# Gated recurrence and ELU layer in one kernel: VectorE's sums read two phases' banks straight from PSUM, and what follows them is put in another order

## The chip, the core and the metric

One core of one Trainium2 chip runs the kernel. Its engines run side by side, each through its own list of instructions in order: TensorE (PE, with its weight loads as PEld), VectorE (DVE), ScalarE (ACT), GpSimd (POOL) and SyncE (SP), which only issues transfers here. The metric is the time of one execution on the device in microseconds (us). Matrix products land in PSUM, eight banks of 128 x 512 fp32 numbers. All else lies in SBUF.

## The reference

For 4 batches, 8 heads, 768 tokens and a head width of 48, a state is carried along the tokens, and its output, 3072 rows of 384 numbers, goes through a two-layer network with an ELU between:

```
f = 1 / (1 + exp(-f_logit))
state = 0
for t in range(768):
    state = f[t][:, None] * state + outer(k[t], v[t])
    y[t] = q[t] @ state
x = y as 3072 x 384
h = x @ w_in                                  # 384 x 2048
g = where(h > 0, h, exp(min(h, 0)) - 1)
out = g @ w_out                               # 2048 x 384
```

w_in and w_out arrive as 64-bit floats. The kernel makes fp32 weights of them and also checks their range, since a fast way and a general way share one launch and a flag chooses at the end which result stands.

## The kernel before

The 3072 tokens are worked off in 12 **units** of 256. Units 0 and 1 use plain first products, while the weights are being converted and summed. Units 2 to 11 use a scheme with fewer products, and this is where the change lies.

**A unit in the network.** The 2048 hidden columns are split into four **quads** of 512. A quad's eight blocks of h (four column blocks by two token blocks, each 128 x 128) come out of 20 products of 128 x 128 instead of 24. Each product multiplies a block of x, or a sum of such blocks, by a block of w_in, or a sum of such blocks; the h blocks are then sums and differences of the products. The sums of x blocks (`X_SUMS`, made by `blend`, L939) are made on POOL for each unit from unit 3 on: slots 0 to 7 of the tile `xt` hold x, and the sums fill slots 8 to 15 and then write over some of the first eight. `PHASES` splits a quad's 20 products into five **phases** of 3, 5, 5, 4 and 3 products (tile `psH`, L957). A phase adds into one of the quad's two banks; its last number lists the products as (slot of the bank, slot of x, block of w). After each phase ScalarE copies what is complete into the tile `vals` (L962), 18 blocks of 128 x 128 of which there are two, one for even and one for odd quads. VectorE makes the h blocks from `vals` in seven additions of 128 x 256 (`joins`, L947): four after phase 3, three after phase 4. The two banks go round: the first bank of the next quad is the second bank of this one, and so the next quad's phase 0 waits until phase 3 of this one has been read, and its phase 1 until phase 4 has been.

**ELU and the second product.** A **pair** is half a quad: 256 hidden columns for 256 tokens, eight pairs a unit, two a quad. For a pair ScalarE runs Relu and Exp into a tile `gg` (L970, L971) and VectorE one fused operation that completes the ELU (L990). POOL makes four sums of 128 x 128 from it (tile `sums`, L1000), and PE seven products of 128 x 192 into `psM` (L1049). After a unit's eighth pair VectorE combines the banks of `psM` (L1059) and SP stores.

**The attention** of unit u+1 or u+2 is worked off beside it: ScalarE makes the gates, VectorE scans and reciprocals (L685, L690), POOL scales k and q by them (L680), PE has short products (`psT`, `psU`, `psS`, `psY`), VectorE masks (L776) and adds up states (L749), ScalarE copies the unit's x into `xt` (L837, L839).

**What sets the order.** It is written out by hand. The loop at the end runs over **steps** of two phases each, ten a unit, here called s0 to s9; time T counts half steps. In each step it issues what `plan` holds for T, the two phases and their joins, what `plan` holds for T + 1, some products of the second layer (`take`, as many as `CHUNKS` says), and the exponentials of a pair. Before the change, the ELU operations due come first in a step; a quad that ends in step s has the exponentials of its first pair at the end of step s and of its second at the end of s + 1, and each pair's ELU at the start of the step after. Quads end in s2, s4, s7 and s9. `BL`, `A3`, `D4` place a unit's x sums, attention and decays within the unit before. Each engine's list is the order of issue, so an instruction waits for all that was issued to its engine before it. All waits between engines are semaphores for data or buffers.

Of the kernel before, what the change touches and what calls it, by code (L numbers as in the profile page):

```python
# [8 lines left out]
FP32 = mybir.dt.float32  # L9
# [3 lines left out]
AF = mybir.ActivationFunctionType  # L13
# [343 lines left out]
def fast(ctx: ExitStack, tc: tile.TileContext, q, k, v, f_logit, w_in, w_out, out, flag, outer):  # L357
# [53 lines left out]
    A3 = (3, 7, 11, 13)  # L411
    BL = 15
# [5 lines left out]
        (14, 1, 5, -1), (12, 1, 0, -1), (1, 3, 1, -1), (9, 2, 3, -1), (13, 4, 9, -1), (8, 2, 4, -1),  # L418
        (10, 2, 0, -1), (7, 8, 14, -1), (2, 13, 5, -1), (11, 10, 9, -1), (15, 0, 14, -1), (6, 4, 15, -1),
# [14 lines left out]
    )  # L434
    SEED = (1, 5)
    JOIN3 = (
        (ALU.add, (5, 12), (7, 17), (11, 12)), (ALU.add, (4, 17), (15, 15), (4, 13)),
        (ALU.add, (5, 13), (5, 6), (10, 12)), (ALU.subtract, (7, 14), (11, 13), (8, 14)),
    )
    JOIN4 = (  # L440
        (ALU.add, (8, 15), (0, 1), (3, 12)), (ALU.add, (7, 16), (7, 16), (8, 9)),
        (ALU.subtract, (6, 17), (8, 13), (2, 17)),
    )
    PLACES = ((14, ((1, 1), (1, 0), (0, 0), (0, 1))), (4, ((1, 1), (0, 1), (1, 0), (0, 0))))
# [89 lines left out]
    vals = [cst.tile([128, 18, 128], FP32, name=f"vals{i}") for i in range(2)]  # L534
# [121 lines left out]
    def check(n):  # L656

        if not wide:
            return
        hi = again.pop(n)[:].bitcast(FP32)[:, 1::2]  # L660
        for i, op in enumerate((ALU.min, ALU.max)):
            nc.vector.tensor_reduce(
                out=spans[:, i, n : n + 1], in_=hi, axis=mybir.AxisListType.X, op=op, apply_absolute_value=True
            )
# [270 lines left out]
    def blend(u, e, some=slice(None)):  # L935

        x = xts[u]
        for to, a, b, _ in X_SUMS[some]:
            e.tensor_tensor(out=x[:, to], in0=x[:, a], in1=x[:, b], op=ALU.subtract)  # L939
# [3 lines left out]
    def joins(n, todo):  # L943
        v = vals[n % 2]
        pick = lambda a, b: v[:, a : b + 1 : b - a] if b > a else v[:, a : a + 1].broadcast_to([128, 2, 128])
        for op, to, x, y in todo:
            nc.vector.tensor_tensor(out=pick(*to), in0=pick(*x), in1=pick(*y), op=op)  # L947

    def phase(n, i):
# [12 lines left out]
        nc.scalar.copy(v[:, at : at + size], bank[:, frm : frm + size])  # L962
# [3 lines left out]
    def exped(P, h, where):  # L966
        m, j = order[P]
        g = sb.tile([128, 4, 128], FP32, tag="gg", name=f"gg{m}_{j}", bufs=4)
        gs[P] = g, where
        nc.scalar.activation(g[:], h, AF.Relu, scale=-1.0)  # L970
        nc.scalar.activation(g[:], g[:], AF.Exp, scale=-1.0)  # L971
        phs[P] = h
# [14 lines left out]
    def elu(P):  # L987
# [5 lines left out]
        if m > DIRECT or m == DIRECT and j >= PLAIN:  # L993
            s = ss[P] = sb.tile([128, 4, 128], FP32, tag="sums", name=f"sums{m}_{j}", bufs=3)
# [89 lines left out]
    def finish_flag(part):  # L1084
        if wide and not part:
            ok = fine[:, 0, 0:1]
            nc.vector.tensor_reduce(out=spans[:, 0, 0:1], in_=spans[:, 0], axis=mybir.AxisListType.X, op=ALU.min)
            nc.vector.tensor_reduce(out=spans[:, 1, 0:1], in_=spans[:, 1], axis=mybir.AxisListType.X, op=ALU.max)
            for i, op, limit in ((0, ALU.is_ge, 1.125 * 2.0**-15), (1, ALU.is_lt, 1.875 * 2.0**16)):
# [124 lines left out]
    at_step(BL2, lambda: blend(2, nc.vector, slice(0, 6)), lambda: blend(2, nc.gpsimd, slice(6, 12)))  # L1214
# [46 lines left out]
    CHUNKS = (6, 6, 6, 0, 7, 6, 6, 6, 7, 6)  # L1261

    def exp_pair(n, i):
        frm, where = PLACES[i]
        exped(PLAIN_UP * NP + 2 * n + i, vals[n % 2][:, frm : frm + 4], where)
# [25 lines left out]
    for n, z in exps.pop(5 * total // 2):  # L1291
        exp_pair(n, z)
        elus.setdefault(5 * total // 2 + 1, []).append(lambda n=n, z=z: elu(PLAIN_UP * NP + 2 * n + z))
    for s in sorted(elus):
        for f in elus[s]:
            f()
# [51 lines left out]
```

## Time and profile before

| | |
|---|---|
| runs of the kernel | 624.70, 626.36, 629.08 us; median 626.36 |
| the profiled execution | 624.47 us, its span 622.7 us, mean granted TensorE clock 0.963 |
| units 0 and 1 | until about 120 us |
| units 2 to 11 | from there to the end; the same wait of PE comes back at 168.98, 219.01, ... 368.73, 418.03, ... 516.46, 564.22 us, so a unit takes about 49.4 us |
| busy between 368 and 418 us | PE 44.2, DVE 36.0, ACT 25.9, POOL 28.7 us |
| SP's list | transfers alone |

In the rows of the trace, a matrix product of fp32 numbers stands as two records, and a record is about 0.29 us long, though the next one starts 0.11 or 0.16 us after it: the pace of PE is read from stretches of many records. "L957" is line 957 of the kernel before; the same code stands a few lines further down in the changed one.

### The profile page before, as it was taken

The page shows a single profiled execution, that of the slowest core. Times are in us where ns is not written, and L with a number is a line of the kernel's source. Part 1 is how long each engine was busy: PE and PEld are TensorE (multiplying, and loading weights), DVE is VectorE, ACT ScalarE, POOL GpSimd, SP SyncE. Part 2 cuts the span into 40 slices and gives each one's busy share as a digit, 9 for nine tenths or more (in the row PEclk, how much of TensorE's full clock was granted, in tenths as well). Part 3 has the DMA queues.
Part 4 walks back from the last instruction along what each step waited for, and adds up shares of the span by engine and source line. Part 5 has one row for each costly group of instructions (what it writes and reads, how often), then busy time and mean ns, then how long its engine had stood idle before and what let it go on. Part 6 is the DMA issues. An engine that isn't in the chain of part 4 may idle for free.

```text
span 622.7 us, 15560 instructions
## 1 busy us (share of the span) xinstructions
PE 554.0 (89%) x6294; PEld 510.2 (82%) x6294; DVE 442.0 (71%) x757; ACT 318.9 (51%) x595; POOL 326.4 (52%) x603
## 2 busy tenths in 40 slices
PE   7799999798799889979979889988989988998994
PEld 3477688788798789879869879878879987997993
DVE  8889776967657858767856866776785786754652
ACT  3387933345455634745527535645554473564541
POOL 6603173665842862672583493485386276355342
PEclk9999999989889989989979989999998997999998
DMA  9999840130142062062061133215206202210001
GB/s 207 256 223 274 229 116 2 33 102 22 36 117 78 8 171 78 8 171 79 9 152 48 50 78 108 72 26 153 78 8 172 78 7 65 78 34 1 27 3 31
DMA packets 39474, 54.29 MB, mean 87 GB/s; under 512 B 4032, under 2 KB 29216, under 8 KB 39392
## 3 DMA queue, kind: packets, MB, share of 16 engines
q1 hardware_dynamic: 38592, 52.61, 32.4%
q8 instruction: 51, 0.84, 0.6%
q10 hardware_dynamic: 800, 0.59, 0.4%
q14 instruction: 31, 0.25, 0.1%
HBM read 45.02 MB, written 4.72 MB: 80 GB/s over the span
## 4 chain that ended last, share of the span: by engine, by line
PE 38%; DVE 26%; POOL 13%; ACT 10%; issue 6%; DMA 6%; SPq 1%; ACTq 0%; DVEq 0%; POOLq 0%
PE psM L1049 14%; PE psH L957 14%; DVE vals L947 13%; POOL xt L939 9%; PE psH L980 3%; DVE gg L990 3%; POOL sums L1000 3%; ACT gg L970 2%; DMA f<-f 2%; DVE f L690 2%; ACT vals L962 2%; DVE f L685 2%; ACT gg L971 2%; PE psS L768 1%; PE psU_a L791 1%
## 5 line engine op out<-in xcount | busy, mean ns | idle before, releaser
L1000 POOL TENSOR_TENSOR sums<-gg 128x128 f32<-128x128 f32 x172 | 83.3, 504 | 203.9 <-DVE gg L990 189.4
L947 DVE TENSOR_TENSOR vals<-vals 128x256 f32<-128x256 f32 x280 | 142.1, 519 | 67.0 <-ACT vals L962 59.2
L962 ACT COPY vals<-psH 128x512 f32<-128x512 f32 (+1 forms) x200 | 105.1, 540 | 122.7 <-PE psH L957 121.5
L957 PE MATMUL psH<-xt,wi 128*128 128x128 f32 x880 | 144.7, 286 | 3.5 <-DVE gg L990 3.5
L957 PE MATMUL psH<-xt,area 128*128 128x128 f32 x720 | 128.0, 283 | 12.1 <-ACT vals L962 11.0
L1049 PE MATMUL psM<-area,sums 128*128 128x192 f32 x516 | 112.5, 343 | 28.0 <-POOL sums L1000 28.0
L957 PEld LDWEIGHTS psH<-xt,wi 128*128 128x128 f32 x880 | 125.5, 202 | 3.7 <-DVE gg L990 3.7
L957 PEld LDWEIGHTS psH<-xt,area 128*128 128x128 f32 x720 | 107.7, 197 | 15.7 <-ACT vals L962 13.7
L1049 PEld LDWEIGHTS psM<-area,sums 128*128 128x128 f32 x516 | 89.1, 200 | 31.1 <-POOL sums L1000 31.0
L970 ACT ACTIVATE gg<-vals 128x512 f32<-128x512 f32 x80 | 50.4, 630 | 104.7 <-DVE vals L947 76.0
L990 DVE SCALAR_TENSOR_TENSOR gg<-gg,vals 128x512 f32<-128x512 f32 x80 | 58.2, 728 | 59.6 <-ACT gg L971 51.7
L1049 PE MATMUL psM<-wo,gg 128*128 128x192 f32 x376 | 80.5, 336 | 10.2 <-DVE gg L990 10.2
L1049 PEld LDWEIGHTS psM<-wo,gg 128*128 128x128 f32 x376 | 62.4, 191 | 16.0 <-DVE gg L990 15.2
L939 POOL TENSOR_TENSOR xt<-xt 128x128 f32<-128x128 f32 x114 | 59.9, 553 | 9.2 <-DMA xt<-xt 3.9
L690 DVE RECIPROCAL f<-f 128x256 f32<-128x256 f32 x36 | 62.8, 1747 | 1.1
L971 ACT ACTIVATE gg<-gg 128x512 f32<-128x512 f32 x96 | 60.5, 630 | 3.1
L680 POOL TENSOR_TENSOR k<-k,f 128x256 f32<-128x256 f32 x48 | 37.5, 785 | 36.6 <-DVE f L685 16.1
L680 POOL TENSOR_TENSOR q<-q,f 128x256 f32<-128x256 f32 x48 | 39.0, 813 | 18.7 <-DMA f<-f 15.6
L1000 POOL TENSOR_TENSOR sums<-sums,gg 128x128 f32<-128x128 f32 x86 | 47.1, 548 | 0.0
L980 PE MATMUL psH<-xt,wi 128*128 128x256 f32 x192 | 45.1, 384 | 2.3 <-DVE xt L887 1.7
L1000 POOL TENSOR_TENSOR sums<-gg,sums 128x128 f32<-128x128 f32 x86 | 43.6, 507 | 6.7
L1049 PE MATMUL psM<-area,gg 128*128 128x192 f32 x172 | 43.9, 338 | 0.0
(107 smaller groups left out, 667.6 us busy)
## 6 DMA issues: line engine op xcount, KB each, us to landing
area<-in_moe_w_out_dram SPq DMA_DIRECT2D x8, 768.0 KB, 10.6
again<-in_moe_w_in_dram SPq DMA_DIRECT2D x16, 384.0 KB, 5.4
again<-in_moe_w_out_dram SPq DMA_DIRECT2D x16, 384.0 KB, 3.8
k<-in_k_dram SPq DMA_DIRECT2D x12, 384.0 KB, 4.7
q<-in_q_dram SPq DMA_DIRECT2D x12, 384.0 KB, 5.8
v<-in_v_dram SPq DMA_DIRECT2D x12, 384.0 KB, 6.0
area<-in_moe_w_in_dram SPq DMA_DIRECT2D x8, 576.0 KB, 9.2
out_dram<-o SPq DMA_DIRECT2D x42, 96.0 KB, 1.7
```

The lines of the kernel that those rows point to most:

```text
L680: e.tensor_tensor(out=t[n][:, p], in0=t[n][:, p], in1=t["f"][:, p, "kq".index(n)], op=ALU.mult)
L690: nc.vector.reciprocal(f[:, p, 1], f[:, p, 0])
L939: e.tensor_tensor(out=x[:, to], in0=x[:, a], in1=x[:, b], op=ALU.subtract)
L947: nc.vector.tensor_tensor(out=pick(*to), in0=pick(*x), in1=pick(*y), op=op)
L957: nc.tensor.matmul(bank[:, slot], lhsT=w_block(q, w), rhs=xts[m][:, x], start=(i < 2 and t == 0), stop=True, skip_group_check=True,)
L962: nc.scalar.copy(v[:, at : at + size], bank[:, frm : frm + size])
L970: nc.scalar.activation(g[:], h, AF.Relu, scale=-1.0)
L971: nc.scalar.activation(g[:], g[:], AF.Exp, scale=-1.0)
L980: nc.tensor.matmul(ph[:, i], lhsT=wi[j][:, kt, i * 128 : (i + 1) * 128], rhs=xts[m][:, 2 * kt : 2 * kt + 2].rearrange("n t f -> n (t f)"), ...
L990: nc.vector.scalar_tensor_tensor(out=g[:], in0=g[:], scalar=-1.0, in1=phs.pop(P), op0=ALU.add, op1=ALU.max)
L1000: nc.gpsimd.tensor_tensor(out=s[:, i], in0=x, in1=y, op=op)
L1049: nc.tensor.matmul(pm[bank][:, half * DH : (half + 1) * DH], lhsT=x, rhs=y, start=first, stop=(j == NP - 1), skip_group_check=True,)
```

## The change

- **Fewer copies.** ScalarE copies phases 0, 1 and 2 of a quad and no longer phases 3 and 4. VectorE's additions read these two phases' blocks in PSUM. There are eight additions a quad in place of seven: after phase 3 two of 128 x 256 and one of 128 x 128 with one operand in PSUM (`JOIN3`); after phase 4 one of 128 x 256 and one of 128 x 128 likewise (`JOIN4`); and three of 128 x 256 with both operands in SBUF (`MID`, two, and `LAST`, one). `PHASES`, `SEED` and `PLACES` are rewritten to suit; the sizes of the phases and the count of products stay. `vals` has 13 blocks in place of 18; `gg` has five buffers in place of four, `sums` four in place of three.
- **Order in a step.** The ELU operations come after the step's phases and joins, not ahead of them. Both pairs of a quad that ends in step s have their exponentials at the end of step s + 1 and their ELU in step s + 2. `CHUNKS` is changed with that; the first unit of the scheme takes 42 products of the second layer in its loop where it took 52, and what comes after the last step takes the rest.
- **Sums of x.** Twelve of 128 x 128 become six of 128 x 256, each making two sums. For units 3 to 11 they are issued one per half step from T = 16 to T = 21 after the start of the unit before (the last two in the unit's own first step), where all twelve came at T = 15.
- **Range checks.** Each of the 32 checks was two reductions of 128 x 384 on VectorE (least and greatest magnitude); it is now two activations on ScalarE that add up their results (squares, and an exponential that vanishes for all but tiny numbers), and `finish_flag` has other limits.

```diff
-    A3 = (3, 7, 11, 13)
-    BL = 15
+    A3 = (3, 9, 12, 13)
+    BL = 16
...
     X_SUMS = (
...
+        ((12, 13), (1, 2), (0, 0)), ((10, 11), (2, 2), (3, 4)), ((9, 14), (1, 4), (5, 10)),
+        ((1, 2), (3, 14), (1, 5)), ((8, 15), (0, 13), (9, 10)), ((6, 7), (4, 11), (8, 9)),
     )
...
     PHASES = (
...
+        (0, 1, 0, 3, ((1, 8, 16), (0, 9, 13), (2, 14, 12))),
+        (1, 8, 0, 4, ((0, 5, 4), (3, 3, 6), (1, 5, 14), (1, 1, 7), (2, 0, 15))),
+        (0, 4, 0, 4, ((1, 12, 20), (0, 7, 8), (2, 4, 18), (3, 13, 1), (3, 4, 2))),
+        (1, 0, 0, 0, ((0, 2, 19), (3, 1, 5), (1, 11, 0), (2, 15, 9))),
+        (0, 0, 0, 0, ((0, 6, 17), (2, 10, 11), (3, 13, 3))),
     )
...
     JOIN3 = (
...
+        (ALU.add, (4, 11), (4, 11), 1, (1, 2)), (ALU.add, (0, 12), (4, 9), 1, (0, 3)), (ALU.subtract, 4, 6, 1, 1, True),
     )
...
+    MID = (ALU.add, (1, 5), (1, 5), None, (9, 11)), (ALU.subtract, (8, 9), (5, 5), None, (8, 12))
+    JOIN4 = (ALU.add, (3, 6), (2, 11), 0, (0, 2)), (ALU.subtract, 2, 3, 0, 3)
+    LAST = ((ALU.add, (3, 7), (3, 10), None, (4, 7)),)
...
-        for i, op in enumerate((ALU.min, ALU.max)):
-            nc.vector.tensor_reduce(
-                out=spans[:, i, n : n + 1], in_=hi, axis=mybir.AxisListType.X, op=op, apply_absolute_value=True
-            )
+        nc.scalar.activation(hi, hi, AF.Square, accum_out=spans[:, 1, n : n + 1])
+        nc.scalar.activation(hi, hi, AF.Exp, scale=-(2.0**26), accum_out=spans[:, 0, n : n + 1])
...
-        nc.scalar.copy(v[:, at : at + size], bank[:, frm : frm + size])
+        if size:
+            nc.scalar.copy(v[:, at : at + size], bank[:, frm : frm + size])
...
-        at_step(t + BL, lambda u=u: blend(u, nc.gpsimd))
+        for n in range(6):
+            at_step(t + BL + n, lambda u=u, n=n: blend(u, nc.gpsimd, slice(n, n + 1)))
...
-    CHUNKS = (6, 6, 6, 0, 7, 6, 6, 6, 7, 6)
+    CHUNKS = (7, 7, 7, 7, 0, 6, 6, 6, 5, 5)
...
-        for f in elus.pop(s, ()):
-            f()
         for f in plan.pop(T, ()):
             f()
+        done = []
         for i in (2 * s, 2 * s + 1):
             n, i = divmod(i, 5)
             phase(n, i)
-            if i == 3:
-                joins(n, JOIN3)
-            elif i == 4:
-                joins(n, JOIN4)
-                for z in range(2):
-                    exps.setdefault(s + z, []).append((n, z))
+            if i > 2:
+                joins(n, JOIN3 if i == 3 else JOIN4)
+                done.append((n, MID if i == 3 else LAST))
+        for n, todo in done:
+            joins(n, todo)
+            if todo is LAST:
+                exps[s + 1] = n
+        for P in elus.pop(s, ()):
+            elu(P)
         for f in plan.pop(T + 1, ()):
             f()
-        take((5, 5, 4)[s] if s < 3 else CHUNKS[s % 10])
-        for n, z in exps.pop(s, ()):
-            exp_pair(n, z)
-            elus.setdefault(s + 1, []).append(lambda n=n, z=z: elu(PLAIN_UP * NP + 2 * n + z))
+        take((4, 4, 3, 3)[s] if s < 4 else CHUNKS[s % 10])
+        if s in exps:
+            exp_quad(exps.pop(s), s)
```

Three places show how the lists of the engines change; names end in the unit and, for `gg` and `sums`, the pair. The first is POOL's list around the start of unit 9 (unit 8 still being worked off): `xt9` are sums of unit 9's x blocks, `k0` and `q0` scalings for unit 10, `sums8_4` the sums that pair 4 of unit 8 needs. Before:

```order
L680 TENSOR_TENSOR q0_69<-q0_69,f0_68 128x256
L939 TENSOR_TENSOR xt9_4580<-xt9_4580 128x128 x12
L1000 TENSOR_TENSOR sums8_4_4630<-gg8_4_4626 128x128 x2
L1000 TENSOR_TENSOR sums8_4_4630<-sums8_4_4630,gg8_4_4626 128x128
L1000 TENSOR_TENSOR sums8_4_4630<-gg8_4_4626,sums8_4_4630 128x128
L680 TENSOR_TENSOR k0_70<-k0_70,f0_68 128x256
L680 TENSOR_TENSOR q0_69<-q0_69,f0_68 128x256
L1000 TENSOR_TENSOR sums8_5_4670<-gg8_5_4666 128x128 x2
L1000 TENSOR_TENSOR sums8_5_4670<-sums8_5_4670,gg8_5_4666 128x128
L1000 TENSOR_TENSOR sums8_5_4670<-gg8_5_4666,sums8_5_4670 128x128
```

After, the same place on POOL:

```order
L1005 TENSOR_TENSOR sums8_4_4592<-gg8_4_4569 128x128 x2
L1005 TENSOR_TENSOR sums8_4_4592<-sums8_4_4592,gg8_4_4569 128x128
L1005 TENSOR_TENSOR sums8_4_4592<-gg8_4_4569,sums8_4_4592 128x128
L1005 TENSOR_TENSOR sums8_5_4598<-gg8_5_4572 128x128 x2
L1005 TENSOR_TENSOR sums8_5_4598<-sums8_5_4598,gg8_5_4572 128x128
L1005 TENSOR_TENSOR sums8_5_4598<-gg8_5_4572,sums8_5_4598 128x128
L941 TENSOR_TENSOR xt9_4505<-xt9_4505 128x256
L676 TENSOR_TENSOR q0_69<-q0_69,f0_68 128x256
L676 TENSOR_TENSOR k0_70<-k0_70,f0_68 128x256
L676 TENSOR_TENSOR q0_69<-q0_69,f0_68 128x256
L941 TENSOR_TENSOR xt9_4505<-xt9_4505 128x2x128
L941 TENSOR_TENSOR xt9_4505<-xt9_4505 128x256
```

The sums of both pairs, one sum of x and three scalings now stand ahead of the fifth operation on `xt9` (the row `128x2x128`, which makes slots 8 and 15); before, all twelve stood ahead of the sums.

The second place is VectorE's list where unit 8's last quad ends (s9): `vals1` is its tile, `psH8_3` its banks, `gg8_4` and `gg8_5` the two pairs of the quad before. Before:

```order
L990 SCALAR_TENSOR_TENSOR gg8_4_4626<-gg8_4_4626,vals0_128 128x512
L685 SCALAR_TENSOR_TENSOR f0_68<-f0_68 128x256
L690 RECIPROCAL f0_68<-f0_68 128x256
L662 TENSOR_REDUCE spans_135<-again22_4539 128x1 x2
L990 SCALAR_TENSOR_TENSOR gg8_5_4666<-gg8_5_4666,vals0_128 128x512
L947 TENSOR_TENSOR vals1_129<-vals1_129 128x2x128 x7
```

After, from the same scan on:

```order
L681 SCALAR_TENSOR_TENSOR f0_68<-f0_68 128x256
L686 RECIPROCAL f0_68<-f0_68 128x256
L951 TENSOR_TENSOR vals1_129<-vals1_129,psH8_3_1_4547 128x2x128 x2
L951 TENSOR_TENSOR vals1_129<-psH8_3_1_4547,vals1_129 128x128
L951 TENSOR_TENSOR vals1_129<-vals1_129,psH8_3_0_4526 128x2x128
L951 TENSOR_TENSOR vals1_129<-vals1_129,psH8_3_0_4526 128x128
L951 TENSOR_TENSOR vals1_129<-vals1_129 128x2x128
L951 TENSOR_TENSOR vals1_129<-vals1_129 128x256
L951 TENSOR_TENSOR vals1_129<-vals1_129 128x2x128
L995 SCALAR_TENSOR_TENSOR gg8_4_4569<-gg8_4_4569,vals0_128 128x512
L995 SCALAR_TENSOR_TENSOR gg8_5_4572<-gg8_5_4572,vals0_128 128x512
```

The two ELU operations moved behind all eight additions of the last quad, whose first waits for that quad's phase 3.

The third place is PE's list at the same boundary, from unit 8's last two phases to unit 9's first. Before:

```order
L957 MATMUL psH8_3_0_4603<-xt8_4086,wi_132 128x128 x2
L1049 MATMUL psM8_1_4449<-area_134,sums8_4_4630 128x192
L1049 MATMUL psM8_2_4450<-area_134,gg8_4_4626 128x192
L1049 MATMUL psM8_2_4450<-wo_133,sums8_4_4630 128x192
L1049 MATMUL psM8_0_4448<-wo_133,gg8_5_4666 128x192
L1049 MATMUL psM8_3_4451<-wo_133,gg8_5_4666 128x192
L1049 MATMUL psM8_0_4448<-area_134,sums8_5_4670 128x192
L957 MATMUL psH9_0_0_4718<-xt9_4580,area_134 128x128 x3
```

After:

```order
L961 MATMUL psH8_3_0_4526<-xt8_4021,wi_132 128x128 x2
L1054 MATMUL psM8_0_4400<-area_134,sums8_3_4476 128x192
L1054 MATMUL psM8_1_4401<-area_134,sums8_3_4476 128x192 x2
L1054 MATMUL psM8_2_4402<-area_134,gg8_3_4413 128x192
L1054 MATMUL psM8_2_4402<-wo_133,sums8_3_4476 128x192
L961 MATMUL psH9_0_0_4622<-xt9_4505,area_134 128x128 x3
L961 MATMUL psH9_0_1_4627<-xt9_4505,wi_132 128x128 x2
```

Between the two units PE has five products of the second layer in place of six, of pair 3 in place of pairs 4 and 5, and the first product of unit 9 reads slot 8 of `xt9`.

More of the change, by code (lines that the diff above doesn't have):

```diff
@@ L531, in fast @@
         nc.gpsimd.memset(box[:].rearrange("n (p d) -> n p d", d=64)[:, :, 0:PAD], 0.0)
-    vals = [cst.tile([128, 18, 128], FP32, name=f"vals{i}") for i in range(2)]
+    vals = [cst.tile([128, 13, 128], FP32, name=f"vals{i}") for i in range(2)]
     spare = vals[1][:].rearrange("p n f -> p (n f)")
@@ L933, in combine, with pick, blend @@
                 yield
[L935 removed]
+    def pick(v, at):
+        if type(at) is int:
+            return v[:, at]
+        a, b = at
+        return v[:, a : b + 1 : b - a] if b > a else v[:, a : a + 1].broadcast_to([128, 2, 128])
+    def blend(u, e, some):
         x = xts[u]
[L938 to L939 removed]
+        for to, a, b in X_SUMS[some]:
+            e.tensor_tensor(out=pick(x, to), in0=pick(x, a), in1=pick(x, b), op=ALU.subtract)
     quads = {}
@@ L1259, in take, with exp_quad @@
             next(stream, None)
-    CHUNKS = (6, 6, 6, 0, 7, 6, 6, 6, 7, 6)
-    def exp_pair(n, i):
-        frm, where = PLACES[i]
-        exped(PLAIN_UP * NP + 2 * n + i, vals[n % 2][:, frm : frm + 4], where)
+    CHUNKS = (7, 7, 7, 7, 0, 6, 6, 6, 5, 5)
+    def exp_quad(n, s):
+        for i in range(2):
+            frm, where = PLACES[i]
+            P = PLAIN_UP * NP + 2 * n + i
+            exped(P, vals[n % 2][:, frm : frm + 4], where)
+            elus.setdefault(s + 1, []).append(P)
     elu(PLAIN_UP * NP - 1)
```

39 lines of the change are left out of this document (15 added, 24 removed), and 5 rows, old and new, of the table PHASES.

## The prediction, made before the changed kernel was run

> **What bounds the kernel now.** I read the page first, for its shares and the chain that ended last:
>
> ```profile
> PE 554.0 (89%) x6294; PEld 510.2 (82%) x6294; DVE 442.0 (71%) x757; ACT 318.9 (51%) x595; POOL 326.4 (52%) x603
> ...
> PE 38%; DVE 26%; POOL 13%; ACT 10%; issue 6%; DMA 6%; SPq 1%; ACTq 0%; DVEq 0%; POOLq 0%
> PE psM L1049 14%; PE psH L957 14%; DVE vals L947 13%; POOL xt L939 9%; PE psH L980 3%; DVE gg L990 3%; POOL sums L1000 3%; ACT gg L970 2%; DMA f<-f 2%; DVE f L690 2%; ACT vals L962 2%; DVE f L685 2%; ACT gg L971 2%; PE psS L768 1%; PE psU_a L791 1%
> ```
>
> PE is busiest, but the chain leaves it: VectorE's additions carry 13%, POOL's sums of x 9%. Next the waits, to see what PE lacks:
>
> ```profile
> PE psM L1049 <- POOL sums L1000: 28.0, 10, 4.4
> ...
> PE psH L957 <- ACT vals L962: 11.0, 9, 1.7
> PE psM L1049 <- DVE gg L990: 10.2, 15, 2.4
> ```
>
> PE's largest wait comes ten times, nine of them once a unit; the tenth, and 2.37 us of the third row, lie in the tail, which the timeline shows from the last phase to the last but one pair of products:
>
> ```profile
> 603.65 0.61 PE L957 MATMUL psH<-xt,wi 128*128 128x128 f32 x4
> ...
> 609.88 0.92 PE L1049 MATMUL psM<-wo,gg 128*128 128x192 f32 x4 [2.37 <-DVE gg L990]
> 611.78 2.29 PE L1049 MATMUL psM<-area,sums 128*128 128x192 f32 x6 [0.99 <-POOL sums L1000]
> ...
> 616.57 0.49 PE L1049 MATMUL psM<-area,gg 128*128 128x192 f32 x2
> ```
>
> The timeline of PE gives its place, and the chain in order of time what leads to it:
>
> ```profile
> 368.73 1.45 PE L1049 MATMUL psM<-area,sums 128*128 128x192 f32 x4 [2.80 <-POOL sums L1000]
> ...
> 418.03 0.92 PE L1049 MATMUL psM<-area,sums 128*128 128x192 f32 x4 [2.80 <-POOL sums L1000]
> ```
>
> ```profile
> 408.74 0.73 POOL k L680
> ...
> 412.43 3.78 POOL xt L939 x7
> ...
> 416.74 1.25 POOL sums L1000 x3
> ```
>
> A unit is 49.3 us (418.03 less 368.73). Near its end POOL makes all twelve sums of x, then the sums of pair 4, for which PE waits 2.80 us. What PE can do at best follows from its pace:
>
> ```profile
> 385.98 1.95 PE psM L1049 x12
> 387.94 2.23 PE psH L957 x20
> 390.17 1.08 PE psU_a L791 x64
> 391.24 0.96 PE psS L768 x64
> ```
>
> A product is two records: 0.325 us for psM, 0.223 for psH. With 56 and 80 of them and some 5.5 us of attention a unit holds 41.6 us of PE work, so that up to 7.7 us a unit could go. The boundary between units is the place that decides.
>
> **The change, part by part.** The sum is against the profiled execution's own 624.5 us, which is 1.9 under the median of the runs shown, 626.36.
>
> *Prices on VectorE.* These groups (us busy, mean ns) price it:
>
> ```profile
> L947 DVE TENSOR_TENSOR vals<-vals 128x256 f32<-128x256 f32 x280 | 142.1, 519 | 67.0 <-ACT vals L962 59.2
> L990 DVE SCALAR_TENSOR_TENSOR gg<-gg,vals 128x512 f32<-128x512 f32 x80 | 58.2, 728 | 59.6 <-ACT gg L971 51.7 <-POOL sums L1000 6.1 <-issue 1.8
> L662 DVE TENSOR_REDUCE spans<-again 128x1 f32<-128x384 f32 x64 | 31.4, 531 | 0.0
> L776 DVE TENSOR_TENSOR at<-psS,twice 128x512 f32<-128x512 f32 x24 | 15.5, 686 | 13.3 <-PE psS L768 13.3
> L749 DVE TENSOR_TENSOR state<-psU_a,state 128x192 f32<-128x192 f32 x40 | 14.2, 355 | 5.1 <-PE psU_a L791 3.9
> L1059 DVE TENSOR_TENSOR o<-psM,u 128x384 f32<-128x384 f32 x11 | 6.0, 548 | 0.0
> L685 DVE TENSOR_TENSOR_SCAN f<-f 128x256 f32<-128x256 f32 x36 | 28.8, 806 | 9.0 <-ACT f L673 8.9
> L690 DVE RECIPROCAL f<-f 128x256 f32<-128x256 f32 x36 | 62.8, 1747 | 1.1
> ```
>
> An addition with one operand in PSUM takes 0.355 us for 192 columns and 0.548 for 384, 1.0 ns a column: 0.42 for 256 (bounds 0.355 and 0.548), 0.29 for 128 (by the same line; 0.2 to 0.355). I take the line, since both rows lie on either side. A quad's eight are 3 x 0.42 + 2 x 0.29 + 3 x 0.52 = 3.4 us, where seven took 7 x 0.52 = 3.6. So VectorE gains little by them; the reductions taken away are 31.4 us, but beside other work. The Trainium skill ("VectorE: DVE Perf Modes", Rules for kernel authors) advises to accept one element a cycle on a PSUM operand or to copy it to SBUF first if many operations follow, which speaks against this part; by it nothing would be gained here and the boundary below would be 0.2 us longer, some 2 us in the whole sum.
>
> *ScalarE* loses two copies a quad and gets two activations of 128 x 384 a check:
>
> ```profile
> L962 ACT COPY vals<-psH 128x512 f32<-128x512 f32 x120 | 69.1, 584 | 83.4 <-PE psH L957 83.3
> L962 ACT COPY vals<-psH 128x384 f32<-128x384 f32 x80 | 38.0, 475 | 39.2 <-PE psH L957 38.2
> L971 ACT ACTIVATE gg<-gg 128x512 f32<-128x512 f32 x96 | 60.5, 630 | 3.1
> ```
>
> Less 40 x (0.584 + 0.475) = 42 us; more 64 x 0.55 = 35 (bounds 0.475, the copy of that width, and twice it; adding up has no row). ScalarE is half idle, and the exponentials behind the checks have 4 us in hand before VectorE comes to their ELU. I cost both at nothing; without that cover a check costs 1.1 us. No transfer moves: SP's list reads the same. The bigger `gg` and `sums` free no wait that the trace shows of any size.
>
> *The boundary between units.* What the first product of a unit reads is slot 8 of `xt`, the fifth sum of x. POOL's list has ahead of it the sums of two pairs, a sum of x and three scalings, and the pairs' ELU stand behind the last quad's eight additions, which wait for its phase 3. POOL's prices:
>
> ```profile
> 379.20 0.87 POOL L1000 TENSOR_TENSOR sums<-gg 128x128 f32<-128x128 f32 x2 [3.91 <-DVE gg L990]
> 380.04 0.46 POOL L1000 TENSOR_TENSOR sums<-sums,gg 128x128 f32<-128x128 f32 x1
> 380.57 0.46 POOL L1000 TENSOR_TENSOR sums<-gg,sums 128x128 f32<-128x128 f32 x1
> ...
> 405.81 1.11 POOL L1000 TENSOR_TENSOR sums<-gg 128x128 f32<-128x128 f32 x2 [1.92 <-DVE gg L990]
> 406.88 0.63 POOL L1000 TENSOR_TENSOR sums<-sums,gg 128x128 f32<-128x128 f32 x1
> 407.60 0.52 POOL L1000 TENSOR_TENSOR sums<-gg,sums 128x128 f32<-128x128 f32 x1
> 408.74 0.73 POOL L680 TENSOR_TENSOR k<-k,f 128x256 f32<-128x256 f32 x1 [0.62 <-DVE f L685]
> 409.43 0.72 POOL L680 TENSOR_TENSOR q<-q,f 128x256 f32<-128x256 f32 x1
> ```
>
> A pair's sums take 1.83 us (379.20 to 381.03), or 2.3 with VectorE at work; 128 x 256 takes 0.69 from start to start, which I take for the wide sums of x too (bounds 0.5, half as wide, and 0.9). From the start of s9: phase 3 (four products) done at 0.9; additions to 4.35; first ELU (0.69, uncontended) to 5.05; eight POOL sums 3.66, to 8.7; then one sum of x, three scalings and slot 8, 5 x 0.69 = 3.45, to 12.15. PE has meanwhile seven products of psH (1.57) and five of psM (1.63), to 3.2, and then waits 8.9 us. At the last boundary there are no scalings (no unit 12): 6.8. Nine boundaries: 8 x 8.9 + 6.8 = 78, where nine waits were 27.0 (the 28.0 above less 0.99): **+51**. Low bounds of every price leave 8.0 a wait, high ones 10.2.
>
> *Within a unit.* From the end of s3's products: VectorE combines `psM` (three operations of 192 columns and two of 384, 2.2 us, behind a copy on ScalarE that I put at 0.4), then the eight additions to 6.0, ELU to 6.7, POOL's first sum at 7.15. PE's cover is seven products, psU and psS, eight products: 1.57 + 2.04 + 1.79 = 5.4. It waits 1.8, and 0.4 more for the later sums: 2.2, where the ELU used to stand ahead of the additions. VectorE then has an ELU (0.7), two masks (1.4), the states (1.8), scan and reciprocal twice (5.1), five additions (2.2), two ELU (1.4) and two more additions (0.7), 13.3 us, to 20.0; PE comes at 19.0 to s8's first phase, whose bank those additions free: 1.0. That makes 3.2 in each of units 2 to 9, 2.2 in unit 10 (no scans), 4.4 in unit 11 (no attention to cover): 32, against 11.0 + 10.2 less the 2.37, 18.8: **+13** (bounds: all of these waits gone, -19, and +23 with a us more a unit).
>
> *Clock.* How PE starts again shows in the granted clock (the column behind the counts):
>
> ```profile
> 366.00:371.00 5.00, 2.27 (x9) 0.80 0.39 66
> ...
> 612.00:614.00 2.00, 2.00 (x7) 0.50 0.01 4
> ```
>
> The tail's waits end in some 3 us at half clock, 1.5 lost; the 2.8 us waits lose that in about two boundaries of three (0.80 here). So 0.5 more a boundary: **+4.5** (bounds 0 and 13). The Trainium skill ("TensorE: Matmul & The Clock Gate", Part 1) halves the clock after an idle window of about 3.4 us until as much busy time has passed; taken strictly, no wait of 2.8 us would cost anything now, this term would be 9 x 1.7 = 15 and the time some 701; the 0.80 behind a 2.8 us wait speaks against.
>
> *The ends.* Ten psM products leave the first unit's loop: **-3**. They join the tail, where PE needs 13 us from the last phase (604.2 to 617.2 in the rows above). Afterwards POOL's four pairs of sums end at about 10.8 and the last product at 13.0, with the clock **+0.5**.
>
> Sum: 51 + 13 + 4.5 - 3 + 0.5 = 66; 624.5 + 66 = **690 us**.
>
> **The rivals.**
> 1. *The sums of x come in time (faster).* If slot 8 were ready when PE gets there, the 27 us of waits now would go, with 3 of the ends: 624.5 - 30 = 594. For it: a sum takes 0.7, and one comes per half step. Against: it decides only if POOL reaches that sum by 3.2, and the ELU ahead of POOL's eight sums can't start before 4.3.
> 2. *The middle pays (still slower).* After so long a wait ScalarE and VectorE have caught up; if no wait within a unit is left, 690 - 32 = 658. For it: reductions of 31.4 us are gone from VectorE. Against: VectorE's row of work in s4 to s8 starts from PE's own products, so it can't be ahead of them.
> 3. *About the same.* Rival 2 with the additions hidden too, so that POOL's 7.1 us alone count from phase 3 on: a wait of 4.8, less 37 more: 621. It needs the ELU to run ahead of the additions, against VectorE's list.
> 4. *More contention.* With POOL's 2.3 a pair (+0.9) and VectorE's additions slower by 0.1 to 0.2, 1.2 a boundary and 1.2 a unit: 690 + 22 = 712.
>
> **How the numbers follow.** The order of the lists leaves little room at the boundary, so the forecast has 0.68, rival 2 0.13, rival 4 0.10, rival 1 0.05, rival 3 0.04. The likeliest is 690. The range takes in rival 2 with 8 us of low prices, 650, and rival 4, 712. A measurement of this kernel tells about 1% from no change: faster by more 0.05, within 1% 0.04, slower by more 0.91.
>
> **What would show it.** In the changed profile PE's first psH of each unit waits for POOL's `xt`, nine times, 8 to 10 us (right), or under 3 (wrong, and then the time is near rival 1). PE's waits on `sums` or `gg` in s5 should be about 2 us, on VectorE's `vals` in s8 about 1; none would mean rival 2. Additions on PSUM should read 0.42 and 0.29 us, a check 0.5 to 0.8 a piece, POOL's wide sums 0.7. A unit should take about 56 us. VectorE waiting for ScalarE's exponentials at the boundary would make the cover I gave the checks wrong.

## The result, and the profile after

| | before | after |
|---|---|---|
| median | 625.53 us (624.02 to 629.08, 4 runs) | 676.3 us (674.5 to 677.71, 4 runs) |
| ratio to before, with its 95% interval | 1 | 1.080 (1.075 to 1.086) |
| span of the profiled execution | 622.7 us | 675.9 us |
| its mean granted clock | 0.963 | 0.926 |

The changed kernel is 8.0% slower, 14 us below the point that was predicted. The page after has, as before, the busy time of each engine with its share and the shares of the chain that ended last:

```profile
PE 561.1 (83%) x6294; PEld 513.5 (76%) x6294; DVE 388.8 (58%) x730; ACT 316.5 (47%) x643; POOL 306.8 (45%) x546
...
PE 53%; DVE 23%; POOL 11%; DMA 5%; issue 3%; ACT 2%; SPq 1%; DVEq 0%; ACTq 0%; POOLq 0%
```

VectorE is relieved by 53 us (442.0 to 388.8), as the change set out to do, and yet the span is 53.2 us longer. PE does the same 6294 instructions in 7.1 us more (561.1 less 554.0) and stands still for 114.8 us (675.9 less 561.1) where it was 68.7: 46.1 more. Those two make up the 53.2. What PE waited for, in total, times and the longest:

```profile
PE psH L961 <- POOL xt L941: 79.6, 9, 9.1
PE psM L1054 <- POOL sums L1005: 8.6, 12, 1.4
...
PE psH L961 <- DVE vals L951: 3.3, 11, 1.1
```

One row carries it. Nine waits before a unit's first product, for POOL's sums of x, take 79.6 us. The waits in the middle of the units, 18.8 us before, have become fewer: 8.6 less the 1.37 that lie in the tail, and 3.3, together 10.5. PE's timeline shows a whole unit, with the wait in brackets:

```profile
452.35 1.65 PE L961 MATMUL psH<-xt,area 128*128 128x128 f32 x6 [9.07 <-POOL xt L941]
...
471.48 0.49 PE L1054 MATMUL psM<-wo,sums 128*128 128x192 f32 x2
...
478.05 1.01 PE L1054 MATMUL psM<-area,sums 128*128 128x192 f32 x4 [0.51 <-POOL sums L1005]
...
490.65 0.68 PE L961 MATMUL psH<-xt,wi 128*128 128x128 f32 x4 [0.18 <-DVE vals L951]
...
507.01 1.65 PE L961 MATMUL psH<-xt,area 128*128 128x128 f32 x6 [9.08 <-POOL xt L941]
```

A unit takes 54.66 us (507.01 less 452.35) against 49.3 before, and 9.1 of it is that one wait. The chain in order of time shows what leads to it: when each group began, how long it was, on which engine.

```profile
440.09 0.90 PE psH L961 x8
441.09 0.43 DVE vals L951
...
443.85 0.42 DVE vals L951
444.26 0.62 DVE gg L995
445.01 1.59 POOL sums L1005 x3
...
448.44 0.45 POOL sums L1005
448.90 0.68 POOL xt L941
449.58 0.68 POOL q L676
450.26 0.68 POOL k L676
450.94 0.68 POOL q L676
451.62 0.69 POOL xt L941
```

Read it from the bottom. PE starts at 452.35, when the sum of x that makes slot 8 is done. Ahead of it on POOL stand three scalings, a sum of x and eight sums of two pairs (445.01 to 448.9). These wait for the ELU, the ELU for the eight additions (441.09 to 444.27), and those for the last quad's phase 3. None of the twelve operations ahead of slot 8 on POOL is needed by PE's next product.

### The profile page after: what moved, and what is told of

Same layout as the page of the kernel before. It is cut to its first block, busy times and chain, and to the rows that moved or that the text cites. A ratio compares the mean times of both kernels' runs of the same rounds, so it can differ in the third digit from the quotient of the medians.

```text
span 675.9 us, 15572 instructions
## 1 busy us (share of the span) xinstructions
PE 561.1 (83%) x6294; PEld 513.5 (76%) x6294; DVE 388.8 (58%) x730; ACT 316.5 (47%) x643; POOL 306.8 (45%) x546
## 4 chain that ended last, share of the span: by engine, by line
PE 53%; DVE 23%; POOL 11%; DMA 5%; issue 3%; ACT 2%; SPq 1%; DVEq 0%; ACTq 0%; POOLq 0%
PE psM L1054 23%; PE psH L961 22%; DVE vals L951 12%; POOL sums L1005 7%; DMA area<-in_moe_w_in_dram 4%; DVE gg L995 4%; PE psH L985 3%; DVE f L686 2%; POOL xt L941 2%; PE psY L802 2%; POOL q L676 2%; DVE o L1064 1%; PE psM L1018 1%; ACT area L630 1%; DVE f L681 1%
## 5 line engine op out<-in xcount | busy, mean ns | idle before, releaser
L1005 POOL TENSOR_TENSOR sums<-gg 128x128 f32<-128x128 f32 x172 | 92.7, 558 | 281.5 <-DVE gg L995 238.3
L961 PE MATMUL psH<-xt,area 128*128 128x128 f32 x720 | 137.2, 299 | 81.6 <-POOL xt L941 79.6
L967 ACT COPY vals<-psH 128x512 f32<-128x512 f32 (+1 forms) x120 | 64.9, 550 | 257.1 <-PE psH L961 222.8
L961 PEld LDWEIGHTS psH<-xt,area 128*128 128x128 f32 x720 | 114.4, 210 | 86.0 <-POOL xt L941 83.1
L951 DVE TENSOR_TENSOR vals<-vals,psH 128x256 f32<-128x256 f32 (+1 forms) x160 | 61.4, 384 | 190.6 <-ACT vals L967 121.2
L1054 PE MATMUL psM<-area,sums 128*128 128x192 f32 x516 | 106.2, 335 | 8.6 <-POOL sums L1005 8.6
L1054 PEld LDWEIGHTS psM<-area,sums 128*128 128x128 f32 x516 | 85.0, 192 | 13.6 <-POOL sums L1005 11.3
L951 DVE TENSOR_TENSOR vals<-vals 128x256 f32<-128x256 f32 x120 | 50.9, 438 | 2.0
L995 DVE SCALAR_TENSOR_TENSOR gg<-gg,vals 128x512 f32<-128x512 f32 x80 | 51.7, 686 | 0.8 <-ACT gg L976 0.5
L941 POOL TENSOR_TENSOR xt<-xt 128x256 f32<-128x256 f32 x57 | 41.4, 728 | 4.8 <-PE psH L985 3.3
L1054 PE MATMUL psM<-wo,sums 128*128 128x192 f32 x172 | 43.1, 332 | 0.3
## 6 DMA issues: line engine op xcount, KB each, us to landing
area<-in_moe_w_out_dram SPq DMA_DIRECT2D x8, 768.0 KB, 11.2
```

Of the source, the lines that this page charges most:

```text
L941: e.tensor_tensor(out=pick(x, to), in0=pick(x, a), in1=pick(x, b), op=ALU.subtract)
L951: nc.vector.tensor_tensor(out=pick(v, to), in0=x, in1=y, op=op)
L961: nc.tensor.matmul(bank[:, slot], lhsT=w_block(q, w), rhs=xts[m][:, x], start=(i < 2 and t == 0), stop=True, skip_group_check=True,)
L995: nc.vector.scalar_tensor_tensor(out=g[:], in0=g[:], scalar=-1.0, in1=phs.pop(P), op0=ALU.add, op1=ALU.max)
L1005: nc.gpsimd.tensor_tensor(out=s[:, i], in0=x, in1=y, op=op)
L1054: nc.tensor.matmul(pm[bank][:, half * DH : (half + 1) * DH], lhsT=x, rhs=y, start=first, stop=(j == NP - 1), skip_group_check=True,)
```

## The experiments

Each was timed in three rounds beside the kernel before, whose medians in those four groups of runs were 626.35, 626.94, 626.88 and 625.99 us. The theory was that the place of slot 8 in POOL's list makes the loss and that the other parts of the change gain. The rivals were that the late ELU, or the checks on ScalarE, or the additions on PSUM cost it.

**Sums of x early, all else as changed.** The six sums are issued at half steps 16 to 18 after the start of the unit before, two at each, in place of one at each of 16 to 21:

```diff
-        for n in range(6):
-            at_step(t + BL + n, lambda u=u, n=n: blend(u, nc.gpsimd, slice(n, n + 1)))
+        for n, z in enumerate((0, 0, 1, 1, 2, 2)):
+            at_step(t + BL + z, lambda u=u, n=n: blend(u, nc.gpsimd, slice(n, n + 1)))
```

> All six sums of x at T = 16, 17 and 18, ahead of the pairs' sums of s9 on GpSimd; all else as after. Theory A (the boundary wait is GpSimd's list: slot 8 stands behind two pairs' sums and three scalings): the nine waits of 9.1 us on xt go to none; TensorE then waits about 1 us a boundary for the first pair's ELU and sums, and loses no clock after it (2.4 us each): 676 - 9 x 10.5 = about 582 us, below before. Theory B (the late ELU is what costs; the sums of x only hide it): the wait is renamed to sums or gg and stays above 6 us a boundary: 650 or more.

It took 589.32 us, 0.939 (0.936 to 0.943) of before. Its page and its waits:

```profile
PE 545.6 (93%) x6294; PEld 493.8 (84%) x6294; DVE 394.2 (67%) x730; ACT 315.8 (54%) x643; POOL 308.0 (52%) x546
```

```profile
PE psM L1054 <- POOL sums L1005: 15.6, 21, 1.4
```

The nine waits for `xt` are gone, and PE's own busy time falls by 15.5 us (561.1 to 545.6) with the granted clock at 0.994. So the place of those sums costs 87 us (676.3 less 589.32), and the rest of the change gains 37 (626.35 less 589.32). The changed `A3` and `CHUNKS` were not put back by themselves; a kernel further down that has the old ones waits for `xt` in the same way.

**Only the last two sums moved**, to the same half step as the fourth, ahead of the three scalings:

```diff
-        for n in range(6):
-            at_step(t + BL + n, lambda u=u, n=n: blend(u, nc.gpsimd, slice(n, n + 1)))
+        for n, z in enumerate((0, 1, 2, 3, 3, 3)):
+            at_step(t + BL + z, lambda u=u, n=n: blend(u, nc.gpsimd, slice(n, n + 1)))
```

> Only the fifth and sixth sums of x move, to T = 19, just ahead of the three scalings, still behind the pairs' sums. Theory A: each of eight waits falls by 3 x 0.69 = 2.1 us to 7.0, the ninth stays: 676 - 17 = about 660 us. If scalings are not on the path: 676.

It took 662.79 us, 1.056 (1.051 to 1.060). The wait, as a row of the same view, fell by the three scalings:

```profile
PE psH L961 <- POOL xt L941: 63.3, 9, 7.0
```

16.3 us less over the eight boundaries that have scalings are 2.04 each, or three times 0.68. In what remains, 7 us a boundary, the sum of x still stands behind the sums of the pairs.

**The ELU ahead of the phases and additions of its step**, the sums of x as changed:

```diff
+        for P in elus.pop(s, ()):
+            elu(P)
         for f in plan.pop(T, ()):
             f()
...
-        for P in elus.pop(s, ()):
-            elu(P)
         for f in plan.pop(T + 1, ()):
             f()
```

> The ELU operations go back ahead of a step's phases and additions; the sums of x stay late. Theory A: at the boundary the first ELU starts when its exponentials are done, some 4 us earlier than behind the eight additions, so that the wait falls to about 4.7 us; the additions come 1.3 us later: 676 - 40 = about 636 us. If the additions ahead of the ELU cost nothing there: 676.

It took 645.62 us, 1.029 (1.026 to 1.033): 31 us less than the changed kernel, 10 fewer gained than expected. Its wait for `xt`, and POOL's timeline up to it:

```profile
PE psH L961 <- POOL xt L941: 58.5, 9, 7.1
```

```profile
369.90 1.42 POOL L1005 TENSOR_TENSOR sums<-gg 128x128 f32<-128x128 f32 x2 [2.29 <-PE psH L961]
...
374.43 1.52 POOL L941 TENSOR_TENSOR xt<-xt 128x256 f32<-128x256 f32 x2
...
377.94 1.52 POOL L941 TENSOR_TENSOR xt<-xt 128x256 f32<-128x256 f32 x2
```

The ELU now begins 0.8 us after phase 3 starts, 3.4 us earlier than in the chain above (444.26 against 440.09). But two sums of x stand behind the pairs' sums (374.43, x2) where one stood (448.90), and the pairs' sums, with VectorE adding beside them, take 4.5 us (369.90 to 374.43) in place of 3.9. I had counted neither.

**Wide sums in the kernel before.** Two kernels give the kernel before the six wide sums; the slots of `xt` are renumbered for them. In the first they stay together at half step 15, in the second they are spread over 16 to 21 (the second line in place of the first):

```diff
-        at_step(t + BL, lambda u=u: blend(u, nc.gpsimd))
+        for n, z in enumerate((0, 0, 0, 0, 0, 0)):
+        for n, z in enumerate((1, 2, 3, 4, 5, 6)):
+            at_step(t + BL + z, lambda u=u, n=n: blend(u, nc.gpsimd, slice(n, n + 1)))
```

> The kernel before with one part of the change alone: the twelve sums of x as six of 128 x 256, all at T = 15 as before. Theory A: they take 6 x 0.69 = 4.1 us on GpSimd where twelve took 6.6, and the pairs' sums behind them come 2.5 us earlier, so that the wait of 3.0 us a boundary falls to about 0.5: 626 - 9 x 2.5 - 5 (clock) = about 600 us. If the boundary is bound elsewhere: 626.

> The kernel before with the six wide sums spread over T = 16 to 21, as in the change, and nothing else: ELU operations stay ahead of the additions and one pair to a step. Theory A: slot 8 now stands behind one pair's sums in s9 (1.8 us), a sum and three scalings; worked out from s9's start, ELU to 0.8, sums to 2.7, five operations to 6.1 against PE's 3.5: a wait on xt of 2.5 us or a little more in place of the 3.0 on sums, 626 within 8 us. So spreading alone costs little, and only behind the late ELU does it cost 9 us. If spreading alone explains the loss: 660 or more.

Together they took 612.79 us, 0.979 (0.975 to 0.983); spread, 670.25 us, 1.071 (1.065 to 1.076). The second was expected near 626 and missed by 44. Spread, the kernel before waits for the same thing in the same place, and its timelines of VectorE, POOL and PE show why:

```profile
PE psH L963 <- POOL xt L945: 60.4, 9, 7.0
```

```profile
386.89 4.91 DVE L953 TENSOR_TENSOR vals<-vals 128x256 f32<-128x256 f32 x7
...
393.27 1.02 DVE L996 SCALAR_TENSOR_TENSOR gg<-gg,vals 128x512 f32<-128x512 f32 x1 [0.87 <-ACT gg L977]
...
394.84 0.86 POOL L1006 TENSOR_TENSOR sums<-gg 128x128 f32<-128x128 f32 x2
...
396.61 1.52 POOL L945 TENSOR_TENSOR xt<-xt 128x256 f32<-128x256 f32 x2
...
397.38 1.65 PE L963 MATMUL psH<-xt,area 128*128 128x128 f32 x6 [6.67 <-POOL xt L945]
```

I had thought that the sums of x could stand at half step 20 in the kernel before, because its ELU is ahead of the additions of its own step. But half step 20 is the next unit's s0, and that step's list begins with the ELU of the last quad, which needs all seven additions, two exponentials and then the pair's sums. So spreading alone makes nearly the whole loss, 43 of 50 us, although the ELU keeps its old order. Together at half step 15, the sums in fewer, wider operations gain 2%. They gain less than expected, since the pairs' sums behind them then wait for the ELU: PE's wait for `sums` falls from 28.0 to 11.4 us and that for `gg` rises from 10.2 to 22.8.

**The parts that were left, one by one.** With the sums late, the checks go back to VectorE. With the sums early they go back too, and in another kernel the buffers `gg` and `sums` get their old counts of 4 and 3:

```diff
-        nc.scalar.activation(hi, hi, AF.Square, accum_out=spans[:, 1, n : n + 1])
-        nc.scalar.activation(hi, hi, AF.Exp, scale=-(2.0**26), accum_out=spans[:, 0, n : n + 1])
+        for i, op in enumerate((ALU.min, ALU.max)):
+            nc.vector.tensor_reduce(
+                out=spans[:, i, n : n + 1], in_=hi, axis=mybir.AxisListType.X, op=op, apply_absolute_value=True
+            )
```

> The range checks go back to VectorE as two reductions of 0.53 us; all else as after. Theory A (they lie beside other work on either engine): 676 within 4 us, the nine waits on xt unchanged at 9.1. If ScalarE's checks held up the exponentials ahead of the boundary: 10 us or more less.

> As early_sums with the range checks on VectorE again. If they lie beside other work there too: 589 within 4 us. If VectorE, now 67% busy, is near the path at the unit's end: 31 us of reductions make up to 10 us: 600.

> As early_sums with four buffers of gg and three of sums, as early_copies_back had. If buffers are nothing: 589, and the 30 us between early_sums and early_copies_back are the copies and the additions. If both pairs of a quad at once need them: up to 600, and the rest is the copies.

The first took 675.0 us, 1.077 (1.073 to 1.081), beside 1.080 (1.075 to 1.086) for the change; the second 589.61 and the third 589.49 us, beside 589.32 with early sums alone. Neither part has an effect that can be measured, although the checks move 27.6 us of VectorE's time with the sums late (416.4 with them, 388.8 without): they lie beside other work on either engine.

The next kernel keeps the early sums and the small buffers, but phases 3 and 4 go back to ScalarE's copies and the additions to the seven in SBUF:

```diff
-        (1, 0, 0, 0, ((0, 2, 19), (3, 1, 5), (1, 11, 0), (2, 15, 9))),
-        (0, 0, 0, 0, ((0, 6, 17), (2, 10, 11), (3, 13, 3))),
+        (1, 10, 0, 4, ((0, 2, 19), (3, 1, 5), (1, 11, 0), (2, 15, 9))),
+        (0, 0, 1, 3, ((1, 6, 17), (2, 10, 11), (3, 13, 3))),
...
-    MID = (ALU.add, (1, 5), (1, 5), None, (9, 11)), (ALU.subtract, (8, 9), (5, 5), None, (8, 12))
+    MID = ()
...
-    LAST = ((ALU.add, (3, 7), (3, 10), None, (4, 7)),)
+    LAST = ()
```

> As early_sums, but ScalarE copies phases 3 and 4 again and VectorE's seven additions read SBUF, as in the kernel before (gg with four and sums with three buffers, so that it fits). If reading PSUM saves what the rows say (a copy of 0.6 us ahead of the additions, 0.3 us of additions a quad): the ELU at each quad's end comes about 1 us later, waits grow by some 1 to 2 us a unit: 600 to 610 us. If reading PSUM is worth nothing: 589.

It took 618.99 us, 0.987 (0.983 to 0.991), 9 us above the range that was expected. Against 589.49 with the same buffers, VectorE's reading of the banks is worth 29.5 us. The waits say how, of PE first and then of VectorE: PE waits 27.1 us for the pairs' sums, where with the copies gone it was 15.6. It also waits 12.2 us for the sums of x, eight times, where it did not wait for them at all: on POOL these stand behind the sums of two pairs, and the last four of them begin 2.2 us after the start of the last quad's phase 3 in place of some 1.1. VectorE's additions wait 108.1 us for ScalarE's copies, where they waited 41.5 for copies and 53.2 for PE's own phases.

```profile
PE psM L1058 <- POOL sums L1009: 27.1, 29, 2.6
PE psH L965 <- POOL xt L945: 12.2, 8, 1.5
```

```profile
DVE vals L955 <- ACT vals L971: 108.1, 48, 6.3
```

**Towards a faster kernel.** With early sums PE's largest wait is for the pairs' `sums`. I first let each pair begin with the three products that need `gg` alone, and then spared the first pair of a unit that order:

```diff
-            if j == plain:
+            if m > DIRECT:
+                todo = [todo[i] for i in (0, 1, 5, 3, 4, 2, 6)]
+            elif j == plain:
                 todo = todo[3:] + todo[:3]
```

> As early_sums, but in each pair's seven products of the second layer the three that need only the ELU come first, then those of the first, third, second and fourth sum. Theory A: what is left of TensorE's waits on sums (15.6 us in early_sums, 0.82 and 0.50 a unit) goes nearly to none: 589 - 9 x 1.3 = about 578 us.

> As early_blocks_first, but a unit's first pair keeps its old order, since its first bank is also that of the attention's scores, for whose mask TensorE waited 2.1 us a unit there. Theory: the wait of 0.82 us a boundary on the third sum goes, the 0.50 of the first pair stays: 589 - 9 x 0.8 = about 582 us. If the order of a pair's products does more harm than that (the clock fell in early_blocks_first without long waits): 595 or more.

Both missed: 606.34 us, 0.969 (0.965 to 0.974), and 593.61 us, 0.947 (0.944 to 0.950), neither below early sums alone. In the first a unit's first pair opens with a bank that held attention scores and waits for VectorE to mask them; in the second the remaining wait only grew, from 0.50 to 1.20 us:

```profile
PE psM L1056 <- DVE at L772: 18.8, 9, 2.1
```

```profile
373.76 1.01 PE L1056 MATMUL psM<-area,sums 128*128 128x192 f32 x4 [1.20 <-POOL sums L1005]
```

Why the second is 4 us above early sums is settled only in part: its waits are not longer in total (11.4 us for `sums` in place of 15.6), but PE is busy 5.2 us longer at a clock of 0.989 in place of 0.994. By an estimate from the windows of the trace, some 2.8 us of that are work at half clock at two places, 124 to 131 and 551 to 554 us, where early sums has only one, 127 to 130.

The last kernel joins the two moves that gained, the ELU ahead in its step (as in the diff above) and the sums of x early, three at each of half steps 16 and 17:

```diff
-            at_step(t + BL + n, lambda u=u, n=n: blend(u, nc.gpsimd, slice(n, n + 1)))
+            at_step(t + BL + n // 3, lambda u=u, n=n: blend(u, nc.gpsimd, slice(n, n + 1)))
```

> Sums of x early (three at T = 16, three at T = 17, so that all stand ahead of the pairs' sums) and ELU operations ahead of a step's phases and additions, as in the kernel before. If the late ELU is a cost of its own at the boundary: the wait of 0.82 us on sums at each unit's start and the 0.50 later go, 589 - 9 x 1.3 = about 578. If putting the additions first pays for itself (banks come free 1.3 us earlier): waits on vals of 0.3 to 2 us a unit come back, as in elu_first, and the time is 589 to 600.

It took 575.72 us, 0.920 (0.917 to 0.923): faster than both kernels. Its page and waits:

```profile
PE 540.7 (94%) x6294; PEld 498.4 (87%) x6294; DVE 403.3 (70%) x730; ACT 316.9 (55%) x643; POOL 327.0 (57%) x546
```

```profile
PE psH L961 <- DVE vals L951: 7.6, 15, 2.3
...
PE psM L1054 <- POOL sums L1005: 1.0, 1, 1.0
```

The waits for `sums` that were 15.6 us with early sums are nearly gone, the waits for `vals` have come back as far as 7.6 us from 2.8, and PE is busy for 94% of the span. The 13.6 us below early sums belong to both edits together, since three of the six sums of x stand earlier too.

## Why the prediction was right

Term by term, against the two profiled executions:

| term | predicted | measured |
|---|---|---|
| wait between units, nine times | +51 | +52.6 (79.6 less 27.0) |
| waits within the units | +13 | -8.3 (10.5 less 18.8) |
| PE's busy time, by the clock | +4.5 | +7.1 |
| the ends, and what is left | -2.5 | +1.8 |
| sum | +66 | +53.2 |

That the sum came within 13 us owes a little to luck: the second term was 21 us too high, and the other three were 8.5 us too low together.

*The wait between units* was right in its mechanism and nearly in its size: 9.07 and 9.08 us in the rows above, 8.9 predicted. The steps hold too. The eight POOL sums took 3.9 us (3.66 predicted), and the five operations from the sum of x to slot 8 took 3.4 (3.45). Early sums take the whole wait away, and moving past the scalings takes a fifth of it. One reading was too narrow: the prediction laid the wait to the ELU behind the additions. With the sums spread in the kernel before, where the ELU stands ahead, PE waits 7 us as well. What decides is that slot 8 stands behind any sums of pairs of the last quads, since those hang on PE's own last phases.

*The waits within the units* is the term that was mis-sized. I took 2.2 us in s5 and 1.0 in s8; the rows show 0.51 and 0.18. VectorE's timeline, in the same unit, gives the reason for the first:

```profile
471.06 0.36 DVE L1064 TENSOR_TENSOR o<-psM,u 128x192 f32<-128x192 f32 x1 [5.26 <-ACT u L1065]
...
473.31 0.86 DVE L951 TENSOR_TENSOR vals<-vals,psH 128x256 f32<-128x256 f32 x2
...
476.40 1.29 DVE L995 SCALAR_TENSOR_TENSOR gg<-gg,vals 128x512 f32<-128x512 f32 x2
```

The prediction let VectorE combine the `psM` banks 0.4 us after the end of s3's products. It began 0.75 us ahead of their end (471.06; PE's next product starts at 471.81), since only the last of the four banks is still being written. All of VectorE's row moved forward by 1.15 us. The additions took 3.1 us (473.31 to 476.40; 3.4 predicted), and PE's cover was 5.7 us, from 471.81 to where its wait of 0.51 began, in place of 5.4. So three errors of the same sign turned 2.2 into 0.5. In s8 VectorE freed the bank 18.7 us after 471.81, where I took 20.0, although it stood idle for 1.0 us on the way; PE came after 18.7 us, where I took 19.0. This is what the second rival foresaw in part, but it laid it to VectorE having caught up; and its 658 us would have needed all waits gone and no more lost to the clock.

*The clock* cost more than I took. How PE starts again after the wait, in windows with their length, PE's busy time and records, granted clock, DMA share and GB/s:

```profile
446.00:449.00 3.00, 0.00 (x0) 0.61 0.92 217
449.00:452.00 3.00, 0.00 (x0) 0.50 0.63 206
452.00:454.00 2.00, 1.65 (x7) 0.50 0.04 8
...
456.00:458.00 2.00, 2.00 (x11) 0.78 0.00 0
458.00:460.00 2.00, 2.00 (x18) 1.00 0.33 38
```

The wait begins at 443.28 (452.35 less 9.07). By the mean of the first window the clock is halved at about 446.7, some 3.4 us later, and by that of 456 to 458 it stays so to about 456.9. So PE works 4.5 us at half clock and loses 2.3 us there. At the other boundaries the granted clock of the 6 us after the wait gives 2.2 to 2.5, and 1.7 at the last. The prediction took 1.5, and 1.0 for the waits of before. The rule of the Trainium skill that the prediction weighed ("TensorE: Matmul & The Clock Gate", Part 1) agrees with the 3.4 us into the wait; its end after as much busy time would lose 1.7 a boundary, the trace shows 2.3. Its total of 15 did not come, 7.1 did, since the shorter waits of before had already cost PE its clock: in the 12 us that follow them it was 0.75 to 0.87 in seven cases and 1.00 in two.

*The ends.* PE was ready for unit 3 at 169.66 us (178.74 less its wait of 9.08). Before, it began unit 3 at 175.86, which is 172.6 without the wait of 3.23 just ahead: 3.0 less, as predicted, though part of it is PE at half clock behind the wait of before. From the last phase to the last product it was 14.5 us in place of 13.3, 1.2 more in place of 0.5.

*The prices* were near. Groups with total and mean ns:

```profile
L951 DVE TENSOR_TENSOR vals<-vals,psH 128x256 f32<-128x256 f32 x120 | 49.9, 416 | 189.2 <-ACT vals L967 121.2 <-PE psH L961 64.2
L951 DVE TENSOR_TENSOR vals<-psH,vals 128x128 f32<-128x128 f32 x40 | 11.6, 291 | 1.4
L951 DVE TENSOR_TENSOR vals<-vals 128x256 f32<-128x256 f32 x120 | 50.9, 438 | 2.0
L659 ACT ACTIVATE again<-again 128x384 f32<-128x384 f32 x32 | 17.8, 558 | 0.0
```

Predicted were 0.42, 0.29, 0.52 and 0.55 us. Giving the move of the checks no price was right, and the runs with the checks put back show it. The Trainium skill ("VectorE: DVE Perf Modes", Rules for kernel authors) leaves two ways for a PSUM operand, to read it at one element a cycle or to copy it first if many operations follow. Each block has only one or two additions to follow here, and the run with the copies put back shows that reading it directly is 29.5 us faster.

The first rival, sums of x in time, came out at 589 us when it was made true (594 predicted), so its condition was wrong and its price near. The price was partly luck: PE's busy time fell by 8.4 us as well (554.0 to 545.6), which the rival did not count, while 0.82 us of waiting a boundary stayed. The third, about the same, and the fourth, more contention, did not come about: the pairs' sums on POOL took 176.7 us in all, where they took 174.0 before, and the additions were shorter (0.44 us and less in place of 0.52).

## What to carry to other kernels

An engine works through its list in order, so an operation that needs nothing late becomes late if it is put behind one that does: ask of each consumer that bounds the kernel what stands ahead of its producer, on that engine, and what each of those waits for in turn. Spreading work over steps is safe only up to the step in whose list such late work begins; here moving five of the six sums of x forward, by one to three half steps, made the difference between 589 and 676 us. A change that loses as a whole can hold a gain: without the one bad place the same edits are 6% faster than the kernel before, and with the ELU moved as well 8%.

## What the chip showed that was not expected

A short wait can slow the work after it, and whether it does hangs on when it falls. In the first kernel that began its pairs with `gg` a wait of 2.09 us is followed, about a microsecond after PE had begun again at 333.92, by some 3.4 us at half clock, although PE worked without a pause from 334 on (the windows have the columns above):

```profile
332.00:334.00 2.00, 0.08 (x1) 1.00 0.39 154
334.00:336.00 2.00, 2.00 (x10) 0.77 0.00 0
336.00:338.00 2.00, 2.00 (x44) 0.50 0.00 0
338.00:340.00 2.00, 2.00 (x47) 0.87 0.03 8
```

That is 1.7 us of lost work in such a place. The wait of 2.09 us comes nine times, but in the 5 us that follow it the granted clock is 0.66 in six cases and 1.00 in three, those whose waits end at 148.09, 193.59 and 381.19. The trace shows in what they differ. The clock falls behind the six at 239.52, 287.32, 335.10, 427.26, 475.00 and 522.84 us, which are 14, 14, 27, 14 and 14 steps of 3.413 us apart, and each time it stays down for one such step. If these steps are carried through the run, each of the six waits (they end at 239.26, 286.63, 333.92, 426.88, 474.44 and 521.73) lies whole within one step, and each of the other three is cut in two by the end of a step (at 147.4, 191.7 and 379.5). In the changed kernel the clock is down from 446.64 to 456.88, three such steps: PE came back in the middle of the second and worked through the third as well, which makes the 4.5 us above.

Between that kernel and early sums, 11.2 of the 15.2 us by which the span grew (588.1 to 603.3) are PE's busy time (545.6 to 556.8), and the other 4.0 are time in which it stood still (42.5 to 46.5). The Trainium skill ("TensorE: Matmul & The Clock Gate", Part 1) speaks of an idle window of about 3.4 us before the clock is halved; here 2.09 us was enough in six cases of nine, and the measurement decides.

An activation that also adds up its row leaves a second row, a read of the accumulator, of 0.18 to 0.19 us behind the activation's 0.56. And an addition of 256 columns with one operand in PSUM (416 ns) was no dearer than one with both in SBUF (438 ns here, 510 with the copies put back).
